# Threshold attention and a hash-routed mixture of experts: one of the seven products by quarters, sums kept in PSUM, attention's transfers in other steps

## The chip, the cores and the metric

The kernel runs on one core of a Trainium2 chip. The metric is the device time of one execution in microseconds (us); less is better. The engines are TensorE (PE in the profile; its weight loads PEld), VectorE (DVE), ScalarE (ACT), GpSimd (POOL) and SyncE (SP), which here only issues DMAs.

## The reference

Two blocks in a row, in fp32. Attention with a threshold: B=8, H=8, S=576, D=64; only scores within tau of a row's largest count. Its output, 4608 rows of 512, goes through a layer of 8 experts, each 512 to 1024 with ReLU and back to 512. The token's id alone says which expert gets it.

```python
scores = scale * np.matmul(q, k.transpose(0, 1, 3, 2))
thresh = np.max(scores, axis=-1, keepdims=True) - tau
scores = np.where(scores >= thresh, scores, -1000000000.0)
attn = np.exp(scores - np.max(scores, axis=-1, keepdims=True))
attn = attn / (np.sum(attn, axis=-1, keepdims=True) + 1e-09)
x = np.matmul(attn, v)                        # then (B,H,S,D) to (B*S, H*D)
expert_idx = token_ids * np.int64(2654435761) % np.int64(E)
for e in range(E):
    mask = expert_idx == e
    h = np.maximum(x[mask] @ w1[e], 0.0)
    out[mask] = h @ w2[e]
```

## The kernel before, in words

**Attention** (0 to some 480 us) goes over 32 pairs of heads (p), each in five steps (s = 0 to 4), in one hand-written order: a loop over n = 5p + s (L710) issues the work of several pairs at once. For step n it scores (`score`, PE, L235), negates with a row maximum (`negate`, DVE, L246, and on POOL the threshold `thr`, L253), exponentiates (`expo`, ACT, L260) and masks (`mask`, DVE, L271). Two steps later the weights are transposed on PE (`turn_w`, L282) and copied by ACT (`put_wT`, L303). The product with v follows for the pair before (`av_part`, L313). For a finished pair, POOL adds epsilon to the row sums at s = 1 (`add_eps`, `rec`, L343), DVE takes the reciprocal at s = 2 (L740), and at s = 0, two pairs late, `put_xm` multiplies (DVE, L352) and SP writes the rows to x_scratch in DRAM by three DMAs (L358, L363). Each engine runs its own instructions in this order.

Between these run POOL's indirect transfers. `scatters` (L542) writes the 36 columns of token ids to their slots, one at each step but s = 1. Once the slots are known, `fetch_early` gathers 15 blocks of the first expert's rows (`gather`, L119: 5 tiles of rows, three of the four column blocks of 128 each), at steps 3 and 4 and at the start of step 0 (L714, L803), from n > G0 = 130. The fourth column block is gathered in five transfers after the last pair. SP loads the first experts' weights at s = 2 of pairs 20, 22, 24 and 26.

**Experts** (some 500 us to the end) take one of eight after the other, with capacities of 544 tokens (expert 0), 576 (1 to 4) and 600 (5 to 7). Expert 0's first layer runs during the end of attention (`early_h`, L640; `late_h`, L658 to L664, of which the last tile, fo = 5, lies in a buffer of `ps_m`). All other layers are products of 2 by 2 blocks computed with seven products instead of eight (`seven`, L931): layer 1 in two groups g of output rows (`layer1`), layer 2 at once (`layer2`). `left` and `right` make the sums of blocks on DVE (L858, L861). A product (L941) is 4 (layer 1) or 8 (layer 2) matmuls into each half of a pair of PSUM banks; each matmul shows as two records of the profile[...]. `bank2` hands out four such pairs of banks in turn. Each product is followed by one operation that empties its banks: ACT copies the first to SBUF (`p1`, L951), and DVE adds each of the others to a running sum in SBUF (`u2`, `u3`, `u4`) or to an output (L861); ReLU is ACT's (L948).

After certain products `side1` (layer 1) or `side2` (layer 2) issues the work around: sums for the next layer, squares of the gathered rows (`turn_x`, DVE transposes and then 16 DMAs on SP that move them to xT), `fetch` of the expert after next (POOL gathers), the outputs (`put_squares`: a DVE transpose, L1033, then a POOL scatter of each square, L1042) and the weight loads. After each of those transfers `pause` makes POOL copy a small tile twice (L1027). The last expert's layer 2 covers 480 of its tokens; the last 120 are `last_tile` (L990, L994), with `put_out` (L1009 to L1021) in between.

The tile pools count buffers; the order of instructions on each engine is the program's own (`manual_schedule`), and waits between engines are derived from who writes and reads a tile.

Of the kernel before, what the change touches and what calls it, by code (L numbers as in the profile page):

```python
# [9 lines left out]
FP32 = mybir.dt.float32  # L10
# [3 lines left out]
AF = mybir.ActivationFunctionType  # L14
# [6 lines left out]
def kernel(  # L21
# [12 lines left out]
    nc = tc.nc  # L34
# [109 lines left out]
    with tc.tile_pool(name="a_q", bufs=1) as a_q, \  # L144
# [525 lines left out]
        LAST = NS * NP  # L670
        G0 = NS * ((HP - 1) * B + 2)
        early = [(kt, hp) for kt in range(KT) for hp in range(HP - 1)]
# [15 lines left out]
        with tc.manual_schedule():  # L688
# [21 lines left out]
            for n in range(LAST + NS + 1):  # L710
                p, s = divmod(n, NS)
                m = n - 2
                if s == 0:
                    fetch_early(n)  # L714
                if s == 0 and p + 2 < NP:
# [81 lines left out]
                if 0 < n <= LAST:  # L797
                    for j in range(heads(n - 1)):
                        mask(n - 1, j)
                if s != 1 and placed:  # L800
                    next(scatter_pieces, None)
                if s > 2:
                    fetch_early(n)  # L803
                if n == LAST:
                    fill(1)
# [21 lines left out]
    with tc.tile_pool(name="m_x", bufs=1) as m_x, \  # L827
         tc.tile_pool(name="m_o", bufs=3) as m_o, \
         tc.tile_pool(name="m_s", bufs=1) as m_s:
# [7 lines left out]
        nc.gpsimd.memset(oT[:, :, CAP:SL], 0.0)  # L837
        o_end = m_x.tile([P, DIN], FP32, name="o_end")
        mark = m_x.tile([P, 1], FP32, name="mark")
        w1_s = m_s.tile([P, 3, C2, F2], FP32, name="w1_s")  # L840
        CH = CAP // 2
        x_s = m_s.tile([P, 3, C2, CH], FP32, name="x_s")
        w2_s = m_s.tile([P, 3, FH, D2], FP32, name="w2_s")
        h_s = m_s.tile([P, 3, FH, CH], FP32, name="h_s")
        halves = [m_s.tile([P, 2, CH], FP32, name=n) for n in ("p1", "u2", "u3", "u4")]
        CHL = 32 * (NB - 4) // 2

        ps_m = ctx.enter_context(tc.tile_pool(name="ps_m", bufs=2, space=PSUM))
        turn = [0]

        def bank2():
            turn[0] ^= 1
            if turn[0]:
                return ps_sc.tile([P, 2, 512], FP32, name="sc")
            return ps_m.tile([P, 2, 512], FP32, name="bank2")

# [30 lines left out]
        def w2_sums(e):  # L887
            t = triple(w2_s, 0, FH)
            return t if e == E - 1 else [dealt(x, C2) for x in t]

# [18 lines left out]
        def sums_w2(e):  # L909
            s1 = None  # L910
            if e == E - 1:
                spare = w_pool.tile([P, CO, F], FP32, name="w1_sb")
                s1 = w_tiles["s1"] = spare[:, :, 0:D2]
            return left(*w2_blocks(e, w_tiles[e, 2]), w2_sums(e), s1)

# [9 lines left out]

        def seven(a, a_s, b, b_s, m0, outs, relu, after):

            (a11, a12, s1, a22), (s2, s3, s4) = a, a_s
            (b11, t1, b21, b22), (t2, t3, t4) = b, b_s
            c11, c12, c21, c22 = outs  # L930
            n_k, width, dealt_out = a11.shape[1], b11.shape[2], len(a11.shape) == 4  # L931
            p1, u2, u3, u4 = (t[:, :, 0:width] for t in halves)

            def product(x, y):
                ps = bank2()
                for i in range(2):
                    c0 = m0 + P * i
                    for c in range(n_k):
                        lhsT = (x[:, c, :, i] if dealt_out else
                                x[:, c, c0:c0 + P])  # L940
                        nc.tensor.matmul(ps[:, i, 0:width], lhsT=lhsT, rhs=y[:, c],  # L941
                                         start=c == 0, stop=c == n_k - 1)
                return ps[:, :, 0:width]

            def out(c, ps, u, step):
                add(c, ps, u)()
                if relu:
                    nc.scalar.activation(c, c, AF.Relu)  # L948
                after(step)

            nc.scalar.copy(p1, product(a11, b11))  # L951
            out(c11, product(a12, b21), p1, 0)
            add(u2, product(s2, t2), p1)()
            after(1)
            add(u3, product(s3, t3), u2)()
            after(2)
            out(c21, product(a22, t4), u3, 3)
            k5 = product(s1, t1)
            add(u4, k5, u2)()
            out(c22, k5, u3, 4)  # L960
            out(c12, product(s4, b22), u4, 5)

        def layer1(e, side):

            w, half = w_tiles.pop((e, 1)), caps[e] // 2
            for g in range(NG):
                outs = [h_0[:, FH * i + 2 * g:FH * i + 2 * g + 2, half * k:half * k + half]
                        for i in range(2) for k in range(2)]
                seven(w1_blocks(w), triple(w1_s, 0, C2), x_blocks(e), triple(x_s, 0, C2, half), 2 * P * g,
                      outs, True, lambda step: side(g, step))  # L970

        def layer2(e, side):

            w, half = w_tiles[e, 2], half2(e)
            outs = [oT[:, C2 * i:C2 * i + C2, half * k:half * k + half]
                    for i in range(2) for k in range(2)]
            a = w2_blocks(e, w)
            if e == E - 1:
                a[2] = w_tiles["s1"]
            seven(a, w2_sums(e), h_blocks(0, FH, half),  # L980
                  triple(h_s, 0, FH, half), 0, outs, False, side)

        def last_tile(middle):

            w, o_sb, idx = w_tiles[E - 1, 2], o_end, gidx[:, KT - 1:KT]
            rows = CAP - 2 * CHL
            for c0, c1 in ((0, DIN - P), (DIN - P, DIN)):
                ps = bank2()
                for fo in range(FO):
                    nc.tensor.matmul(ps[0:rows, 0, 0:c1 - c0], lhsT=h_0[:, fo, 2 * CHL:CAP],  # L990
                                     rhs=w[:, fo, c0:c1], start=fo == 0, stop=fo == FO - 1)
                    if (c0, fo) == (0, FH - 1):
                        middle()
                nc.scalar.copy(o_sb[0:rows, c0:c1], ps[0:rows, 0, 0:c1 - c0])  # L994
            put_rows(o_sb[0:rows], idx[0:rows])

        def put_out(e, *groups):
# [14 lines left out]
            for tr, kts in zip(trs, groups):  # L1012
                for i, kt in enumerate(kts):
                    rows = rows_of(kt)
                    o_sb = m_o.tile([P, DIN], FP32, name="o_sb")
                    dst = o_sb[0:rows].rearrange("p (c r q) -> p r c q", c=CO, r=2)
                    src = tr[0:rows, :, D2 * i:D2 * i + D2].rearrange("p r (c q) -> p r c q", c=CO)
                    if e == E - 1 and kt % 2:
                        nc.vector.tensor_copy(dst, src)
                    else:  # L1020
                        nc.scalar.copy(dst, src)  # L1021
                    put_rows(o_sb[0:rows], gidx[0:rows, kt:kt + 1])

        def pause():

            for _ in range(2):
                nc.gpsimd.tensor_copy(stok_odd[:], stok[:])  # L1027

# [48 lines left out]
        with tc.manual_schedule():  # L1077
            run(sums_w2(0), 4)
            fill(18)
            late_h(lambda fo: (ps_sc.tile([P, 2, 512], FP32, name="sc") if fo in (2, 4) else  # L1080
                               ps_m.tile([P, 2, 512], FP32, name="bank2")))
            fetch(1)
            run(sums_h(0, 0, FH), 4)

        with tc.manual_schedule():
            for e in range(E):
                more = e + 1 < E
                turns = turn_x(e + 1) if more else []

                if e > 0:  # L1090
                    w2_work, h_work = sums_w2(e), sums_h(e, 0, 2)

                    def side1(g, step):
                        if g == 0:
                            run(w2_work)
                            if step == 0:
                                put_squares(e - 1, 1)
                        else:
                            run(h_work)
                        if step > 2:  # L1100
                            run(turns, 1 if g == 0 else 2)

                    layer1(e, side1)
                    run(sums_h(e, 2, FH), 4)
                x_work = (sums_w1(e + 1) + sums_x(e + 1)) if more else []

                def side2(step):
                    if step == 0:
                        run(turns, len(turns))
                    else:  # L1110
                        run(x_work, 2)
                    if step == 2 and e + 2 < E:
                        fetch(e + 2)
                    if step == 4 and e + 2 < E:
                        load_w1(e + 2)
                    if more and step == 3:
                        put_squares(e, 0)
# [23 lines left out]
        with tc.For_i(0, n_ov, 1) as it:  # L1141
# [23 lines left out]
            for fo in range(FO):  # L1165
                nc.tensor.matmul(o_ps[:, 0], lhsT=h_0[:, fo, 0:P], rhs=w2_sb[:, fo],
                                 start=(fo == 0), stop=(fo == FO - 1))
            o_sb = m_o.tile([P, DIN], FP32, name="o_sb")
            nc.scalar.copy(o_sb[:], o_ps[:, 0])
# [35 lines left out]
```

## Time and profile before

| | us |
|---|---|
| median of 3 runs | 918.26 |
| lowest, highest | 918.19, 919.33 |
| profiled execution, its own time | 926.27 |
| its span, first to last instruction | 924.6 |
| outside the span | 1.7 |

The profiled execution takes 8.0 us more than the median, so durations are read from it and the result is compared with the median. The granted TensorE clock is 0.999 over the span.

A row of the timeline gives start, duration, engine, line, operation, output and inputs with their shapes, and in brackets how long the engine stood before it and what released it. Neighbouring instructions of one kind are drawn together (x16). A row of busy time by stage gives the length of the stage and the busy time of PE, PEld, DVE, ACT and POOL in it, then the clock, the share of the DMA engines and GB/s. Matmul ends are modelled in the profile, so products are timed here from start to start.

The stages (busy us):

| stage, us | PE | DVE | ACT | POOL |
|---|---|---|---|---|
| 0 to 460, attention | 449.45 | 444.82 | 390.48 | 214.93 |
| 460 to 500, change-over | 39.72 | 19.00 | 10.34 | 9.64 |
| 600 to 650, experts | 50.00 | 36.65 | 5.39 | 38.86 |
| 850 to 900, experts | 50.00 | 32.43 | 7.38 | 40.33 |
| 900 to 925, the end | 17.71 | 3.95 | 1.91 | 9.81 |

### The profile page before, as it was taken

Reading aid. Unit: us, or ns where it says so; the run is one execution under the profiler, and the core shown is the slowest. Engines: PE = TensorE matmul, PEld = TensorE weight load, DVE = VectorE, ACT = ScalarE, POOL = GpSimd, SP = SyncE. Lnnn points to the kernel's source line nnn. Section 1 sums busy time; section 2 is a strip of 40 time slices with the busy share of each in tenths; the row PEclk is TensorE's granted clock in tenths of the full one; section 3 lists DMA queues with packets and bytes.
Section 4 is the critical chain, followed back from the end, with each engine's and each line's share of the span. In section 5 each row is a group of like instructions: output and inputs, shape, how many; then the busy total and the mean of one; then the engine's idle time right before and its main releaser. Section 6 shows DMA issues by size and latency. Waiting matters only on the chain.

```text
span 924.6 us, 21039 instructions
## 1 busy us (share of the span) xinstructions
PE 906.9 (98%) x7495; PEld 661.6 (72%) x7495; DVE 759.9 (82%) x1654; ACT 457.3 (49%) x741; POOL 550.1 (59%) x842
## 2 busy tenths in 40 slices
PE   7999999999999999999999999999999999999997
PEld 4666666656666666565668879788887978879785
DVE  8999999999999999999945696867768685786741
ACT  6888888888888898788922020110202011020210
POOL 4233432456666623446414588787787877878773
PEclk9999999999999999999999999999999999999999
DMA  7454463554545668734011636445252543522001
GB/s 175 95 146 123 107 152 96 134 134 101 124 100 149 167 164 220 209 96 108 16 33 56 195 118 185 136 125 196 63 199 90 170 155 90 218 61 67 28 28 62
DMA packets 114777, 113.13 MB, mean 122 GB/s; under 512 B 32475, under 2 KB 89315, under 8 KB 114672
## 3 DMA queue, kind: packets, MB, share of 16 engines
q1 hardware_dynamic: 105168, 92.64, 37.0%
q0 software_dynamic: 9072, 18.91, 6.6%
q8 instruction: 61, 1.00, 0.4%
q14 instruction: 44, 0.36, 0.1%
q10 hardware_dynamic: 432, 0.21, 0.1%
HBM read 81.99 MB, written 21.44 MB: 112 GB/s over the span
## 4 chain that ended last, share of the span: by engine, by line
PE 83%; POOL 6%; issue 4%; DVE 3%; ACT 2%; DMA 1%; SPq 0%; POOLq 0%; DVEq 0%; ACTq 0%
PE bank L941 18%; PE av L313 18%; PE sc L941 18%; PE sc L235 14%; PE tr L282 11%; POOL out_dram L1042 4%; PE sc L640 3%; POOL stok_odd L1027 2%; PE av L282 1%; DVE ns L246 1%; DVE w L271 1%; ACT w L260 1%; DMA k_sb<-in_k_dram 1%; ACT wT_b L303 1%; PE bank L658 0%
## 5 line engine op out<-in xcount | busy, mean ns | idle before, releaser
L260 ACT ACTIVATE w<-ns,nmx 128x576 f32<-128x576 f32 x288 | 220.4, 776 | 28.6 <-DVE ns L246 27.9
L271 DVE SCALAR_TENSOR_TENSOR w<-ns,thr,w 128x576 f32<-128x576 f32 x288 | 225.7, 816 | 0.0
L253 POOL TENSOR_SCALAR thr<-nmx,drop 128x2 f32<-128x2 f32 (+1 forms) x160 | 104.4, 652 | 188.9 <-DVE ns L246 179.1
L246 DVE TENSOR_SCALAR_CACHE_REDUCE ns<-sc 128x576 f32<-128x576 f32 x288 | 205.7, 746 | 8.5 <-PE sc L235 7.7
L235 PE MATMUL sc<-k_sb,q 64*128 64x288 f32 (+1 forms) x1280 | 178.2, 422 | 1.1 <-DVE ns L246 0.6
L282 PEld LDWEIGHTS tr<-ident,w 64*128 64x128 f32 x2624 | 105.6, 138 | 96.9 <-ACT wT_b L303 35.3
L1042 POOL DMA_INDIRECT out_dram<-o_q,qidx x127 | 139.7, 1100 | 57.8 <-issue 49.2
L282 PE MATMUL tr<-ident,w 64*128 64x64 f32 x2624 | 139.2, 230 | 7.7 <-ACT wT_b L303 4.8
L1027 POOL COPY stok_odd<-stok 128x152 int32<-128x152 int32 x314 | 139.9, 445 | 10.0
L948 ACT ACTIVATE h<-h 128x576 f32<-128x576 f32 (+1 forms) x56 | 38.8, 693 | 142.8 <-DVE h L861 142.0
L235 PEld LDWEIGHTS sc<-k_sb,q 64*128 64x128 f32 (+1 forms) x1280 | 92.2, 177 | 23.5 <-DVE ns L246 9.8
L313 PE MATMUL av<-wT_a,v 128*64 128x320 f32 (+1 forms) x704 | 100.4, 418 | 0.2
L303 ACT COPY wT_a<-tr 128x512 f32<-128x512 f32 (+1 forms) x128 | 81.7, 638 | 20.6 <-PE tr L282 20.1
L303 ACT COPY wT_b<-tr 128x512 f32<-128x512 f32 (+1 forms) x128 | 81.3, 635 | 18.2 <-PE tr L282 10.2
L313 PE MATMUL av<-wT_b,v 128*64 128x256 f32 x640 | 83.2, 389 | 0.0
L313 PEld LDWEIGHTS av<-wT_a,v 128*64 128x64 f32 x704 | 43.7, 136 | 29.0 <-DVE xm L352 0.7
L951 ACT COPY p<-bank 128x576 f32<-128x576 f32 (+2 forms) x11 | 7.0, 634 | 107.5 <-PE bank L941 102.5
L313 PEld LDWEIGHTS av<-wT_b,v 128*64 128x64 f32 x640 | 40.2, 136 | 18.8 <-issue 0.7
L119 POOL DMA_INDIRECT xg<-x_scratch,gidx_x x35 | 41.8, 1193 | 19.2 <-issue 9.3
L542 POOL DMA_INDIRECT slot_scratch<-tok,slot_i x36 | 44.9, 1247 | 9.5 <-issue 7.6
L951 ACT COPY p<-sc 128x576 f32<-128x576 f32 (+2 forms) x11 | 7.0, 637 | 84.7 <-PE sc L941 79.8
L941 PE MATMUL bank<-h,w_sb 128*128 128x288 f32 (+3 forms) x192 | 48.1, 404 | 0.0
(198 smaller groups left out, 1402.4 us busy)
## 6 DMA issues: line engine op xcount, KB each, us to landing
w_sb<-in_moe_w_dram SPq DMA_DIRECT2D x16, 2048.0 KB
q<-in_q_dram SPq DMA_DIRECT2D x62, 288.0 KB
v<-in_v_dram SPq DMA_DIRECT2D x32, 256.0 KB
x_scratch<-xm SPq DMA_DIRECT2D x32, 256.0 KB
xT<-xq SPq DMA_DIRECT2D x84, 80.0 KB
k_sb<-in_k_dram SPq DMA_DIRECT2D x31, 144.0 KB
k_sb<-in_k_dram SPq DMA_DIRECT2D x32, 112.0 KB
x_scratch<-xg SPq DMA_DIRECT2D x9, 256.0 KB
```

The costliest lines, as they stand in the source:

```text
L235: nc.tensor.matmul(sc[out_rows, i, 0:S2], lhsT=q_sb[rows, h, q0:q1], rhs=k_sb[rows, h], start=True, stop=True)
L246: nc.vector.tensor_scalar(out=ns[:].rearrange("p (i s) -> p i s", i=2), in0=sc[:, :, 0:S2], scalar1=-1.0, scalar2=None, op0=ALU.mult, op1= ...
L253: nc.gpsimd.tensor_scalar(out=thr[:, 0:j + 1], in0=stats[n][0][:, 0:j + 1], scalar1=drop[:], scalar2=None, op0=ALU.add)
L260: nc.scalar.activation(w, nss[n, j][:], AF.Exp, bias=stats[n][0][:, j:j + 1], scale=-1.0)
L271: nc.vector.scalar_tensor_tensor(out=w, in0=nss.pop((n, j))[:], scalar=stats[n][1][:, j:j + 1], in1=w, op0=ALU.is_le, op1=ALU.mult, accum_ ...
L282: nc.tensor.transpose(dst[:, r, 64 * c:64 * c + 64], src[rows, c0:c0 + P], ident[rows, rows])
L303: nc.scalar.copy(dst, tr[:, :, 0:64 * n_c].rearrange("p r (c q) -> p r c q", c=n_c))
L313: nc.tensor.matmul(av[64 * j:64 * j + 64, g, c0:c1], lhsT=v_sb[:, c, 64 * j:64 * j + 64], rhs=wT[g][:, i, c0:c1], start=(c == 0), stop=stop)
L542: nc.gpsimd.indirect_dma_start(out=slot_dram[c % 2][:, :], out_offset=bass.IndirectOffsetOnAxis(ap=slot_i[:, c:c + 1], axis=0), in_=tok[:, ...
L941: nc.tensor.matmul(ps[:, i, 0:width], lhsT=lhsT, rhs=y[:, c], start=c == 0, stop=c == n_k - 1)
L1027: nc.gpsimd.tensor_copy(stok_odd[:], stok[:])
L1042: inst = nc.gpsimd.indirect_dma_start(out=rows[:, :], out_offset=bass.IndirectOffsetOnAxis(ap=idx, axis=0), in_=o_sb, in_offset=None, boun ...
```

## The change

**Quarters.** For experts 1 to 7 the second product of each layer, a12·b21, is itself computed with seven products of its quarters (class `Quarters`), in both groups of layer 1 at once. It takes the place of one product in layer 2 and of one in each group of layer 1. Inner sums of the weights (`wi_s`, 128x256 each) and of the inputs (`bi_s`) are made on DVE by the same `left` and `right`. Since layer 2's weights lie in an interleaved order, ACT first copies the block into four quarters (`copy_quarters`, `w2_q`). Expert 0 keeps the plain second product.

**Sums in PSUM.** A class `Seven` takes the place of `seven`. The running sums stay in the banks: u2 = p1 + s2·t2, u3 = u2 + s3·t3 and c21 = u3 + a22·t4 are added by matmul in bank x, and s1·t1 and s4·b22 in bank z. Where a partial sum is needed elsewhere, ACT copies it out before the next matmul adds to the bank (`p1`, `u2`, `mid`); c21 goes to its place by ACT, with ReLU in layer 1. DVE is left with three additions in place of seven for one `Seven`, and one more for c11 where the second product comes by quarters. Four pairs of banks are held from the start of the experts (`banks`) and are handed to the sums by name; the order of the products, and what `side1` and `side2` issue between them, is written anew. Expert 0's layer 2 opens in banks[3], which is the buffer of `late_h`'s last tile.

**Attention's transfers.** Scatters go at steps 0 to 3, not at 0 and 2 to 4. Gathers of the first expert go at steps 2 and 3, from n > G0 = 125, and what remains of the 15 goes all at once at n = 155 (the last pair's step 0); three are left by then.

**Smaller parts.** `pause` copies once and not twice. The output tiles of the end are the buffers of the gathered rows (xg), and the pool m_o is gone. The first squares of an output go out at `side2`'s step 4 and not 3, those of expert 0 in the first layer of expert 1.

```diff
-        G0 = NS * ((HP - 1) * B + 2)
+        G0 = NS * ((HP - 1) * B + 1)
...
-                if s == 0:
-                    fetch_early(n)
...
-                if s != 1 and placed:
+                if s < NS - 1 and placed:
                     next(scatter_pieces, None)
-                if s > 2:
+                if s in (2, 3):
                     fetch_early(n)
+                if n == LAST - NS:
+                    while early:
+                        fetch_early(n)
...
-        def seven(a, a_s, b, b_s, m0, outs, relu, after):
...
-            nc.scalar.copy(p1, product(a11, b11))
-            out(c11, product(a12, b21), p1, 0)
-            add(u2, product(s2, t2), p1)()
-            after(1)
-            add(u3, product(s3, t3), u2)()
-            after(2)
-            out(c21, product(a22, t4), u3, 3)
-            k5 = product(s1, t1)
-            add(u4, k5, u2)()
-            out(c22, k5, u3, 4)
-            out(c12, product(s4, b22), u4, 5)
+        class Seven:
...
+            def keep_p1(self):
+                nc.scalar.copy(self.p1, self.x)
...
+            def u2_sum(self):
+                products(self.x, self.a[4], self.b[4], False)
+                nc.scalar.copy(self.u2, self.x)
...
+            def u3_sum(self, keep):
+                products(self.x, self.a[5], self.b[5], False)
+                if keep:
+                    nc.scalar.copy(self.mid, self.x)
+
+            def c21(self):
+                products(self.x, self.a[3], self.b[6], False)
+                if self.relu:
+                    nc.scalar.activation(self.outs[2], self.x, AF.Relu)
+                else:
+                    nc.scalar.copy(self.outs[2], self.x)
+
+            def c12(self, mid=None):
+                products(self.z, self.a[6], self.b[3], False, mid)
+                self.out(self.outs[1], self.z, self.u2)
...
+        class Quarters:
...
+            def p1_p2(self):
+                products(self.x, self.a[0], self.b[0], True)
+                nc.scalar.copy(self.p1, self.x)
+                products(self.y, self.a[1], self.b[2], True)
+
+            def c11(self):
+                add(self.outs[0], self.y, self.p1)()
+
+            def p5_u2(self):
+                products(self.z, self.a[2], self.b[1], True)
+                nc.scalar.copy(self.p5, self.z)
+                products(self.x, self.a[4], self.b[4], False)
+                nc.scalar.copy(self.u2, self.x)
+
+            def c12_c22(self):
+                products(self.z, self.a[6], self.b[3], False)
+                add(self.outs[1], self.z, self.u2)()
+                products(self.x, self.a[5], self.b[5], False)
+                add(self.outs[3], self.x, self.p5)()
+
+            def c21(self):
+                products(self.x, self.a[3], self.b[6], False)
+                nc.scalar.copy(self.outs[2], self.x)
...
+            q = quarters_of(e, 1, *banks[1:])
+            g0, g1 = group(0, banks[0], banks[2]), group(1, banks[1], banks[3])
+            g0.first()
+            g0.keep_p1()
+            side(0)
+            q.p1_p2()
+            q.c11()
+            g0.u2_sum()
+            side(1)
+            q.p5_u2()
+            g0.s1_t1(True)
+            side(2)
+            q.c12_c22()
+            side(3)
+            g0.u3_sum(False)
+            q.c21()
+            g0.c22(g0.x)
+            side(4)
+            g0.c12()
+            g0.c11(g0.p1)
+            g1.first()
...
+            g1.c11(g1.x)
+            g1.relus()
+            g0.c21()
+            side(6)
+            g1.u2_sum()
...
+            o = Seven(a, w2_sums(e), h_blocks(0, FH, half), triple(h_s, 0, FH, half), 0, outs,
+                      False, *((banks[0], banks[1]) if e else (banks[3], banks[2])))
+            o.first()
+            o.keep_p1()
...
+            q = quarters_of(e, 2, *(banks[i][:, 0:1] for i in (2, 3, 3)))
+            q.p1_p2()
+            q.c11()
+            run(inner_b(second_blocks(e, 2)[1]), 4)
+            o.u2_sum()
+            q.p5_u2()
+            side(0)
+            o.u3_sum(True)
+            side(1)
+            q.c12_c22()
+            o.s1_t1(False)
+            side(2)
+            q.c21()
+            o.c11(o.p1)
+            o.c22(o.z)
+            o.c21()
+            side(3)
+            o.c12(lambda: side(4))
...
         def pause():
 
-            for _ in range(2):
-                nc.gpsimd.tensor_copy(stok_odd[:], stok[:])
+            nc.gpsimd.tensor_copy(stok_odd[:], stok[:])
```

## The prediction

> **What bounds the kernel now.** I read the busy shares and the chain of the page first, then busy time by stage, then the timeline at the places that the edits touch. On the page:
>
> ```profile
> PE 906.9 (98%) x7495; PEld 661.6 (72%) x7495; DVE 759.9 (82%) x1654; ACT 457.3 (49%) x741; POOL 550.1 (59%) x842
> PE 83%; POOL 6%; issue 4%; DVE 3%; ACT 2%; DMA 1%; SPq 0%; POOLq 0%; DVEq 0%; ACTq 0%
> L1027 POOL COPY stok_odd<-stok 128x152 int32<-128x152 int32 x314 | 139.9, 445 | 10.0
> ```
>
> TensorE is 98% busy and 83% of the chain. POOL's copies are 140 us of work, but they are not what ends the program, as the last fence shows. Busy time by stage (columns: sum, then PE, PEld, DVE, ACT, POOL) says how exclusive TensorE is in the experts:
>
> ```profile
> 600.00:650.00 50.00, 50.00 (x208) 42.84 (x207) 36.65 (x43) 5.39 (x8) 38.86 (x57) 1.00 0.48 151
> 850.00:900.00 50.00, 50.00 (x213) 41.20 (x213) 32.43 (x39) 7.38 (x11) 40.33 (x66) 1.00 0.09 28
> ```
>
> 50.00 of 50 us: no product waits there, DVE has a quarter of its time free and ACT nearly all. So TensorE time removed from the experts is time removed from the program, unless a new wait takes its place. How a product is priced, and how soon a bank is emptied:
>
> ```profile
> 608.63 0.74 DVE L861 TENSOR_TENSOR h<-sc,u 128x576 f32<-128x576 f32 x1
> ...
> 612.99 4.04 PE L941 MATMUL bank<-h,w_sb 128*128 128x288 f32 x16
> ...
> 613.24 0.64 ACT L951 COPY p<-sc 128x576 f32<-128x576 f32 x1 [2.46 <-issue]
> ...
> 616.87 1.38 PE L941 MATMUL sc<-h_s,w_s 128*128 128x288 f32 x5
> ```
>
> A layer-2 product starts at 612.99, the next at 616.87: 3.88 us for 16 records, 0.2425 us each. The copy of the product before starts 0.25 us after its successor does and takes 0.64. The sum that ended at 609.37 had begun 1.5 us after its bank was full (607.17), behind other DVE work: today that delay costs nothing.
>
> In attention POOL's gathers matter:
>
> ```profile
> 388.43 1.02 POOL L119 DMA_INDIRECT xg<-x_scratch,gidx  x1 [0.30 <-issue]
> 389.49 0.81 POOL L253 TENSOR_SCALAR thr<-nmx,drop 128x1 f32<-128x1 f32 x1
> 389.89 0.58 ACT L303 COPY wT_b<-tr 128x512 f32<-128x512 f32 x1 [1.81 <-PE sc L235]
> 390.53 0.39 PEld L282 LDWEIGHTS tr<-ident,w 64*128 64x128 f32 x10 [2.03 <-ACT wT_b L303]
> 390.53 0.52 PE L282 MATMUL tr<-ident,w 64*128 64x64 f32 x10 [1.58 <-ACT wT_b L303]
> ```
>
> The transposes that ACT needed were issued at 387.46, but its copy starts only at 389.89, 0.4 us after the end of a gather that was issued at the start of step 0, right behind one from the end of step 4, and TensorE stands for 1.58 us. The same happens at 434.9 (1.64). The end:
>
> ```profile
> 915.80 1.91 PE L990 MATMUL sc<-w_sb,h 128*120 128x128 f32 x16
> ...
> 917.75 0.27 ACT L994 COPY o_end<-sc 120x128 f32<-120x128 f32 x1 [1.27 <-PE sc L990]
> 918.32 1.03 POOL L1042 DMA_INDIRECT out_dram<-o_end,gidx  x1 [0.81 <-issue]
> ```
>
> TensorE's last product, one copy, one transfer: POOL has had nothing else to do for 0.8 us.
>
> **What the Trainium skill says.** (1) "TensorE: Matmul & The Clock Gate", section "Step-by-step: what each phase is for": back to back, a matmul costs its moving columns, and weights are loaded ahead of it. The trace agrees: 300 columns take 0.2525 us, 288 take 0.2425, 272 take 0.229, 128 take 0.109 (L990), near 0.842 ns a column with no visible fixed part. (2) The same page, "LDWEIGHTS (loading the stationary operand)": a load takes its columns over 1.2, so an estimate of 107 ns for 128 columns. The trace's nearest is L990: 120 columns keep up with 0.109 us. (3) "PSUM — Partial Sum Buffer", "PSUM: the matmul accumulator": a matmul that does not open a group adds to what lies in the bank, and a synchronised read in between is allowed. The kernel before never does this, so its trace cannot confirm it; it is what makes part 2 possible, and the synchronisation is its price. (4) "DMA: Bandwidth & Descriptors", "Anatomy of one DMA — SWDGE (gpsimd) path": some 2 us of every transfer is completion. The trace's case is on SP and longer: x_scratch is issued at 477.83 and the gather behind it starts at 481.39.
>
> **The change part by part.** The sum is made on the profiled execution: 926.27 us, span 924.6, 1.7 around it. The median of the runs is 918.26, 8.0 less, and I carry that difference over unchanged.
>
> *1. Quarters.* From expert 1 on, a12·b21 of each layer (3.88 us at 288 columns; two groups of 1.94 in layer 1) becomes seven products of an eighth of it: 28 records x 144 columns x 0.842 = 3.395. Saved 0.485; 0.505 at 300 columns; 0.404 at 240. Widths are 288 for experts 1 to 4, 300 from 5, 240 in the last layer 2: 8 x 0.485 + 5 x 0.505 + 0.404 = **6.8 us**. Bounds: if the weight load sets the pitch, 0.107 (estimate) to 0.117 (0.109 x 128/120) is still under 0.121, so I take 6.8 in full. The new sums (DVE, for each layer 4 of weights, 4 of inputs, 4 of outputs, at about 0.2 to 0.45 by their widths) stand against four removed sums of 0.75 in each of three sevens: about 8 us added and 8.4 removed in 54 us, so DVE stays at some 75%. ACT gains a copy of w2 and up to nine copies, about 15 us in 54, free time.
>
> *2. Sums kept in PSUM.* A product that adds to a bank must wait until ACT has copied the partial sum out: 0.25 + 0.64 + 0.06 restart (ACT copy to PE in attention, 0.06) = 0.95, or 1.00 with a weight load not taken ahead. At three places of an expert (u2 of layer 1's first group, u2 and u3 of layer 2) only two quarter products lie between, 2 x 0.485 = 0.97. Elsewhere a product of 1.94 or more lies between. Bounds per place 0 (a wait cannot gain) to 0.1; I take 0.03 x 21 = **0.6 us lost**. Behind the wait stand all later products, since TensorE keeps their order. Banks that DVE must empty: I laid the new order out with these durations and find the narrowest covers at 0.5 (bank of the first quarter product), 0.9 (second group's first product) and 1.0 us; I take nothing, and price the contrary below.
>
> *3. Expert 0.* Its layer 2 now opens in the bank of the last late_h tile, which DVE reads at 501.83 for 0.72; TensorE would start at 502.6 and not at 501.63: 1.0. The transfers of xT to expert 1 on SP move back by 2.2 us, since the squares run behind more sums; they take 10.5 us to issue and land about 0.4 before the need (0 to 2). The squares of expert 0 now lie in layer 1 of expert 1 ahead of a quarter sum: 0.3. Together **1.3 lost** (1 to 3). In the last expert, cover is 0.81 against a chain of 0.86 to 0.93, and 120-column records may be bound by weights at 0.109 to 0.117, not 0.101: **0.3 lost** (0.2 to 0.6).
>
> *4. One pause.* 157 copies x 0.445 = 70 us leave POOL. It sets no end in the experts, so nothing; squares, gathers and output tiles only come free earlier.
>
> *5. Attention transfers.* Scatters leave the end of step 4 and get a place in step 1; gathers leave step 4 and the start of step 0. Starts of xm give 13.9 us for a plain pair; the nine pairs with scatters take 4.0 more in sum. I credit **2.5** (0 to 4), as the one now in step 1 stands behind rec and thr on POOL, ahead of nothing urgent. The gather pairs take 16.3, 13.9, 14.7 and 15.2, 4.5 over; with gathers in steps 2 and 3 alone I credit **3.5** (2 to 4.5). Against that, three gathers now stand together at the start of the last pair, and the first must wait for x_scratch of two pairs before. In the kernel before:
>
> ```profile
> 447.96 0.82 DVE L352 TENSOR_TENSOR xm<-av,rec 128x640 f32<-128x640 f32 x1
> ...
> 450.50 0.54 POOL L343 TENSOR_SCALAR rec<-rs 128x9 f32<-128x9 f32 x2
> ...
> 452.27 0.21 DVE L740 RECIPROCAL rec<-rec 128x10 f32<-128x10 f32 x1
> ```
>
> xm ends at 448.8; three DMAs on SP (the tail's 477.83 to 481.39 shows up to 3.6 us until a gather) put the first gather at 451.7 to 452.3. Three at the tail's pitch of about 1.6 end near 456.6. thr of the next step and rec of the pair queue behind them on POOL, so rec comes at 457.2 and DVE's reciprocal, due at 452.27, with the masks behind it, waits **5.0** (2.4 to 6); DVE is 97% busy in attention and TensorE follows it. Net **+1.0 gained** (-3 to +5). load_w1, load_w2 and load_pair keep their places on SP.
>
> Sum: 6.8 - 0.6 - 1.3 - 0.3 + 1.0 = 5.6. Profiled execution about 920.7; median 918.26 - 5.6 = **912.7**.
>
> **The rivals.** *DVE late at the banks (slower).* A bank that TensorE needs again is emptied by a DVE sum, and DVE runs in order; the trace shows such sums starting up to 1.46 us after the bank is full, behind a sum of 1.24. With fixed banks that is TensorE time at the first quarter product, at the second group's u2 and at the quarter outputs. It decides from (5.6 + 1.8)/7 = 1.06 us an expert. At two such places of 0.8 each, 11.2 us: 918.26 - 5.6 + 11.2 = **923.9**. For it: DVE at 73%, nearly 30 sums an expert in a new order; against it: covers of 0.5 to 1.0 in my layout, and long sums dealt out step by step.
> *The gathers of the last pair are hidden.* If masks can run ahead or the transfers land early, the 5.0 stays away: 918.26 - 10.6 = **907.7**. Against: reciprocal stands in order ahead of the masks.
> *The products do not shrink.* If 28 short records are paced by weight loads at 0.139 us (3.88/28), part 1 gives nothing: 918.26 + 1.2 = **919.5**. Against: L990's 0.109.
> *Attention loses.* Low credits (2) and 6 at the last pair: 4 worse than nothing, 5 worse than forecast, **917.7**.
>
> **How the numbers follow.** A measurement here can tell about 0.2% (1.84 us) from no change. Likeliest case 912.7, with 909.5 to 915.5 for the bounds of parts 2, 3 and 5: 0.53. Gathers hidden, 906 to 909.5: 0.20. Attention loses or products do not shrink, 916.4 to 920.1: 0.13. DVE late or another wait of that size, over 920.1: 0.14. So faster 0.73, same 0.13, slower 0.14. The range runs from 906.5 to 919.5, leaving out the slower case and little else.
>
> **What would show it.** Right: quarter records every 0.121 us, PE busy about 6.8 us less in the experts, gaps of under 0.1 us ahead of u2, one gap near 1 us at 502, no gap at the starts of pairs 26 to 30, one of 3 to 5 us near 452 to 457 on DVE. Wrong: PE gaps released by DVE sums in each expert, quarter records above 0.13 us, or a last pair without a stall. The forecast fails most easily in part 5, where the loss is an extrapolation.

## The result and the profile after

The changed kernel takes 920.28 us (median of 20 runs, 918.83 to 923.09), the kernel before beside it 918.43 (20 runs, 917.62 to 919.68). The ratio is 1.0019 (95% interval 1.0012 to 1.0026): 1.7 us slower (1.1 to 2.4). Forecast were 5.6 us less.

The page of the changed kernel, its busy shares, its chain and its pauses:

```profile
PE 901.5 (98%) x7663; PEld 669.6 (73%) x7663; DVE 758.9 (83%) x1720; ACT 513.9 (56%) x848; POOL 488.5 (53%) x685
PE 50%; POOL 28%; issue 15%; DVE 2%; ACT 2%; SPq 1%; DMA 1%; POOLq 1%; DVEq 0%; ACTq 0%
L1235 POOL COPY stok_odd<-stok 128x152 int32<-128x152 int32 x157 | 69.5, 443 | 0.6
```

TensorE is busy for 5.4 us less than in the profile before, and ACT for 57 us more. Part of the 5.4 is not less work: a later profile of the kernel before (before_third, below) has TensorE busy for 904.2 us and not 906.9, so 2.7 are left. POOL lost 70 us of its copies. The chain's shares have moved to POOL, but that is only the path by which the chain was followed: the time by stage (sum, PE, PEld, DVE, ACT, POOL) still has TensorE at 50.00 of 50.

```profile
600.00:650.00 50.00, 50.00 (x234) 44.18 (x233) 37.12 (x54) 14.11 (x24) 33.37 (x42) 1.00 0.48 151
850.00:900.00 50.00, 50.00 (x248) 42.56 (x247) 25.85 (x37) 13.33 (x25) 29.00 (x38) 1.00 0.08 25
```

The span of this profile is 917.2 us, and 1.6 lie around it: 918.83, the least of its 20 runs and 1.4 below their median. Against the profile before (span 924.6) it seems 7.4 us faster, while the runs say 1.7 slower. That contradiction is the subject of the experiments. The large wait of the changed kernel is where the prediction put it, at the start of the last pair:

```profile
440.76 1.15 SPq L363 DMA_DIRECT2D x_scratch<-xm  x2
...
443.98 1.10 POOL L119 DMA_INDIRECT xg<-x_scratch,gidx  x1 [3.93 <-DMA x_scratch<-xm]
...
446.69 1.01 POOL L119 DMA_INDIRECT xg<-x_scratch,gidx  x1 [0.30 <-issue]
...
447.77 0.53 POOL L343 TENSOR_SCALAR rec<-rs 128x9 f32<-128x9 f32 x2
...
448.34 0.22 DVE L738 RECIPROCAL rec<-rec 128x10 f32<-128x10 f32 x1 [4.45 <-POOL rec L343]
...
449.26 2.01 PE L235 MATMUL sc<-k_sb,q 64*128 64x288 f32 x8 [3.24 <-DVE ns L246]
```

Read it from the bottom: TensorE waits 3.24 us for DVE, DVE waits 4.45 us for POOL's rec, and three gathers on POOL stand ahead of rec, the first of them for 3.93 us behind the transfer of xm.

### The profile page after: what moved, and what is told of

The parts are those of the page before. It is cut to its first block, busy times and chain, and to the rows that moved or that the text cites. A ratio compares the mean times of both kernels' runs of the same rounds, so it can differ in the third digit from the quotient of the medians.

```text
span 917.2 us, 21463 instructions
## 1 busy us (share of the span) xinstructions
PE 901.5 (98%) x7663; PEld 669.6 (73%) x7663; DVE 758.9 (83%) x1720; ACT 513.9 (56%) x848; POOL 488.5 (53%) x685
## 4 chain that ended last, share of the span: by engine, by line
PE 50%; POOL 28%; issue 15%; DVE 2%; ACT 2%; SPq 1%; DMA 1%; POOLq 1%; DVEq 0%; ACTq 0%
PE av L313 18%; POOL out_dram L1250 17%; PE sc L235 15%; PE tr L282 10%; POOL stok_odd L1235 7%; POOL xg L119 4%; PE sc L640 3%; PE av L282 1%; SPq L1280 1%; ACT w L260 1%; DMA k_sb<-in_k_dram 1%; DVE ns L246 1%; POOLq L1250 0%; PE sc L940 0%; PE bank L940 0%
## 5 line engine op out<-in xcount | busy, mean ns | idle before, releaser
L1250 POOL DMA_INDIRECT out_dram<-o_q,qidx x127 | 147.5, 1161 | 114.6 <-DVE o_q L1241 81.5
L253 POOL TENSOR_SCALAR thr<-nmx,drop 128x2 f32<-128x2 f32 (+1 forms) x160 | 101.1, 632 | 176.4 <-DVE ns L246 167.2
L1235 POOL COPY stok_odd<-stok 128x152 int32<-128x152 int32 x157 | 69.5, 443 | 0.6
L940 PE MATMUL bank<-h,w_sb 128*128 128x288 f32 (+4 forms) x248 | 62.0, 402 | 0.0
L940 PEld LDWEIGHTS bank<-h,w_sb 128*128 128x128 f32 x248 | 58.7, 290 | 0.5
L940 PE MATMUL sc<-h_s,w_s 128*128 128x288 f32 (+2 forms) x224 | 56.6, 406 | 0.0
L964 ACT ACTIVATE h<-h 128x576 f32<-128x576 f32 (+1 forms) x42 | 29.0, 692 | 41.3 <-DVE h L867 41.2
L119 POOL DMA_INDIRECT xg<-x_scratch,gidx_x x35 | 44.7, 1278 | 12.3 <-DVE xq L1272 5.3
```

The costliest lines, as they stand in the source:

```text
L119: nc.gpsimd.indirect_dma_start(out=dst, out_offset=None, in_=src, in_offset=bass.IndirectOffsetOnAxis(ap=idx, axis=0), bounds_check=src.sh ...
L253: nc.gpsimd.tensor_scalar(out=thr[:, 0:j + 1], in0=stats[n][0][:, 0:j + 1], scalar1=drop[:], scalar2=None, op0=ALU.add)
L940: nc.tensor.matmul(ps[:, i], lhsT=lhsT, rhs=y[:, c], start=start and c == 0, stop=c == len(lhsTs) - 1, skip_group_check=not start)
L1250: inst = nc.gpsimd.indirect_dma_start(out=rows[:, :], out_offset=bass.IndirectOffsetOnAxis(ap=idx, axis=0), in_=o_sb, in_offset=None, boun ...
```

## Experiments

There are two theories. *A*: the experts give their 4 us, the moved transfers give nothing, because the long pairs of the first profile are not in the timed runs, and the three gathers of the last pair cost 5 to 6. *B*: the moved transfers do gain what the first profile shows, and something else, in the experts, loses it in timed runs. The kernels of one set were timed on one chip, each beside the same runs of the kernel before. Each set had another chip: 11, 13 and 8 on record. For the first measurement no chip is on record.

### First set: the two halves of the change apart

**before_again**: no edit. 

> The kernel before, unchanged, for a second profile. Theory A (the 8 us by which the first profiled execution of before exceeded its runs were stalls of that one execution, in the pairs with gathers and scatters; they hardly exist in the timed runs): span near 917, the pairs with gathers at 13.9 to 14.3 and not 16.3 and 15.2. Theory B (these stalls are there in every execution): span near 924 again with the same long pairs. Both: ratio 1.000 within 0.001.

**before_attn**: the kernel before with

```diff
-        G0 = NS * ((HP - 1) * B + 2)
+        G0 = NS * ((HP - 1) * B + 1)
-                if s == 0:
-                    fetch_early(n)
-                if s != 1 and placed:
+                if s < NS - 1 and placed:
-                if s > 2:
+                if s in (2, 3):
                     fetch_early(n)
+                if n == LAST - NS:
+                    while early:
+                        fetch_early(n)
```

> The kernel before with the three attention edits alone (steps of scatters, steps of gathers, the rest of the gathers at the last pair). Theory A: they give nothing and the three gathers at n = 155 cost 4.5 us of DVE standing plus 1.5 us of lower TensorE clock: about 924.4, ratio 1.0065. Theory B: 8 us gained, 4.5 to 6 lost: about 916, ratio 0.997.

**after_old_attn**: the changed kernel with these lines turned back. 

> The changed kernel with the attention transfers at the steps of before. Theory A: only the experts' 4 us are left: about 914.3, ratio 0.9955 to before. Theory B: the attention's net gain is lost again and the experts cost something in timed runs: about 922, ratio 1.004.

**after_spread**: the changed kernel with

```diff
-                if s in (2, 3):
+                if s in (2, 3) or s == 1 and p in (28, 29, 30):
                     fetch_early(n)
-                if n == LAST - NS:
-                    while early:
-                        fetch_early(n)
```

> The changed kernel with the last three gathers not together at n = 155 but one each at step 1 of pairs 28, 29 and 30, so that all are out before the last pair. Theory A: the stall of 4.5 us and the slow clock behind it are gone: about 914, ratio 0.995. Theory B: 4.5 us less than the changed kernel's 920.3, about 915.8, ratio 0.997, but before's attention would still be 8 us slower in its own profile.

| kernel | median, us | ratio to before | 95% interval |
|---|---|---|---|
| before, in this set | 924.89 | | |
| before_again | 925.84 | 1.001 | 1.0002 to 1.0018 |
| before_attn | 926.91 | 1.0025 | 1.0014 to 1.0036 |
| after_old_attn | 921.39 | 0.9966 | 0.9953 to 0.9979 |
| after_spread | 918.51 | 0.9929 | 0.9913 to 0.9944 |

This time the kernel before took 924.9 and not 918.4, and so the set answers neither theory as written. What it tells is this: the experts alone gain (0.9966); the attention edits as a whole lose (1.0025); and the harmful one among them is that the last three gathers stand together (0.9929 without it). A pair's length is read from one start of xm to the next. In the profile of before_again the nine scatter pairs are together 3.8 us longer than nine plain pairs of 13.9, and the four gather pairs 3.0; the first profile had 4.0 and 4.5. So the long pairs are there where the kernel takes 925 us. They are not made by profiling: the profiled execution took 924.59, as its set's other runs did.

### Second set: the stall of the last pair, and the layers

**after_again**: the changed kernel once more. 

> The changed kernel, unchanged, beside the kernel before on one chip, so that the parts can be summed there. If the parts add up: where before takes 918.4, ratio 1.002 again; where before takes 924.9 (its gather and scatter pairs lengthened), the old steps cost more and the ratio falls to about 0.999, since 0.9966 for the changed kernel with the old steps and 1.0025 for the attention edits alone multiply to 0.999.

Before 918.0 here; 919.51, ratio 1.0019 (1.0012 to 1.0025), the same as at first.

**after_early3**: the changed kernel with

```diff
             for n in range(LAST + NS + 1):
                 p, s = divmod(n, NS)
                 m = n - 2
+                if n == LAST - NS:
+                    while early:
+                        fetch_early(n)
...
                 if s in (2, 3):
                     fetch_early(n)
-                if n == LAST - NS:
-                    while early:
-                        fetch_early(n)
```

> The changed kernel with its three gathers of n = 155 at the beginning of that step, ahead of put_xm of pair 29 in the order, so that they need not wait for its DMAs to x_scratch; still three in a row. If the wait for x_scratch is the cost (3.9 of the 4.45 us for which DVE stood): 0 to 1 us of standing is left, TensorE keeps its clock, about 5 us faster than the changed kernel. If the gathers' own time on POOL is the cost: it stays within 1.5 us of the changed kernel.

915.33 us, ratio 0.9969 (0.9958 to 0.998), 4.2 less than after_again. The timeline of its last pair:

```profile
438.35 1.37 POOL L119 DMA_INDIRECT xg<-x_scratch,gidx  x1 [0.17 <-issue]
439.43 0.82 DVE L352 TENSOR_TENSOR xm<-av,rec 128x640 f32<-128x640 f32 x1
440.02 1.01 POOL L119 DMA_INDIRECT xg<-x_scratch,gidx  x1 [0.30 <-issue]
441.34 1.25 POOL L119 DMA_INDIRECT xg<-x_scratch,gidx  x1 [0.31 <-issue]
...
443.03 0.88 POOL L343 TENSOR_SCALAR rec<-rs 128x9 f32<-128x9 f32 x2
...
444.09 0.37 SPq L358 DMA_DIRECT2D x_scratch<-xm  x1
```

There are still three gathers in a row, but rec comes 4.7 us earlier. Now xm's transfer waits for the gathers, and no engine is seen to wait for it. From the xm of pair 29 to that of pair 30 are 13.32 us, in the changed kernel 18.37: 5.05 more. In before_third (third set) they are 13.33. So the price was the wait for x_scratch and not the gathers' own time. In time the edit gave 4.2 us; the 1 us by which it stays behind the kernels of the third set (0.9969 against 0.9957 and 0.9959) is within the intervals.

**after_plain2**: the changed kernel with

```diff
-            if e == 0:
-                o.second(banks[0])
+            if e >= 0:
+                o.second(banks[2 if e else 0])
```

In this order the first squares of an expert's output leave before its c21 block is written, so that block of the output is not the reference's. 

> The changed kernel with layer 2's second product of experts 1 to 7 plain again (one product of 128x288 and no quarters), sums still in PSUM. By the prediction's price of a quartered layer (0.485 and two waits of 0.03): 3 us slower than the changed kernel. By what its trace shows (layer 2 took 27.03 us, of which 0.32 are four delayed second records, against 27.16 for seven products of 3.88): only 0.9 us slower.

928.99 us, ratio 1.0112 (1.0098 to 1.0127): 9.5 us more than after_again, a miss of both figures, mostly because the edit brought a wait of its own: c21 now comes last, and the next layer's first product needs its bank.

```profile
PE sc L940 <- ACT oT L999: 6.6, 6, 1.2
```

The products tell more than the total. Without that wait layer 2 of expert 2 takes 27.16 us in this kernel, 7 x 3.88, and 27.03 with quarters in the changed one: 0.13 gained, not 0.485. That reading rests on one trace of each.

**after_swap**: after_spread with

```diff
-            q.c21()
-            o.c11(o.p1)
             o.c22(o.z)
             o.c21()
+            q.c21()
+            o.c11(o.p1)
             side(3)
             o.c12(lambda: side(4))
```

> The changed kernel with the last three gathers at step 1 of pairs 28 to 30, and with the last quarter product of layer 2 moved behind a22·t4, ahead of s4·b22. Behind that quarter then stand weights of w_s (loads of about 196 ns) and not of w_sb (308 ns). If the 0.108 us by which the second record of the next product is late comes from the long weight load behind short records: it is gone at this place (0.02 left), 0.09 x 7 = 0.6 us, on top of the 6 us from the gathers. If it comes from the accumulation into the bank: it stays.

939.94 us, ratio 1.0234 (1.0221 to 1.0248). The expectation's premise was mistaken: from this change on, s4 is written in place into w_sb, so the last product has the same strided weights as the one before, and the late record stayed (the product took 3.99 us). The kernel lost time for another reason:

```profile
PE bank L937 <- DVE oT L864: 15.8, 6, 2.7
```

And the timeline of one of the six:

```profile
631.56 2.10 PE L937 MATMUL sc<-xT,w_sb 128*128 128x288 f32 x8
...
633.48 2.21 DVE L1238 STREAM_TRANSPOSE o_q<-oT 128x1152 f32<-128x1152 f32 x1
...
635.54 0.73 DVE L864 TENSOR_TENSOR oT<-bank,u 128x576 f32<-128x576 f32 x1
...
636.33 0.76 PE L937 MATMUL bank<-xT,w_sb 128*128 128x144 f32 x4 [2.66 <-DVE oT L864]
```

The bank of c12 is full at 631.56, when the next product starts; its addition begins at 635.54, behind the sums for the next expert and the squares' transpose, all of which had to wait for the late c11. This is the prediction's slower rival, made by hand: 2.56 to 2.67 us at one bank in each of six experts, 15.8 in sum. That is not all of the 25 us that this kernel takes more than after_spread_again (third set). By the trace's record of the granted clock, it fell to half for 3.4 us after five of the six waits, and TensorE had work then: an estimate of 1.7 us each, 8.5 in sum. A stage with one such fall (the clock is the column after the busy times; without a fall it is 1.00):

```profile
600.00:650.00 50.00, 47.34 (x215) 41.61 (x214) 32.35 (x46) 11.44 (x20) 28.59 (x35) 0.97 0.46 148
```

### Third set: what is the attention worth where before takes 918?

**before_third**: no edit. 

> The kernel before, for a profile beside the others of this call, since its time was 918.0 to 918.4 in two sets of runs and 924.9 in another. If its pairs with scatters and gathers are what differs: with a median near 918 they take hardly more than 13.9 us each (sum of excess under 2), with a median near 925 they show 7 to 8 us of excess as in the first profile; the experts take 390.1 from expert 1 on in either.

**before_spread**: before_attn with after_spread's edit. 

> The kernel before with attention's new steps but the last three gathers at step 1 of pairs 28, 29, 30 in place of the last pair: what the moved transfers are worth by themselves. Theory A at a median of before near 918: within 1.5 us of before; at one near 925: 4 us faster (0.9929/0.9966). Theory B: 6 us faster in either.

**after_spread_again**: after_spread. 

> The changed kernel with the last three gathers at step 1 of pairs 28 to 30. Experts' 4.0 us and what before_spread shows: at a median of before near 918, 0.9950; near 925, 0.993.

**after_old_again**: after_old_attn. 

> The changed kernel with the attention transfers at the steps of before: the experts' part alone, 4.0 us by the traces, ratio 0.9957 wherever it runs.

| kernel | median, us | ratio to before | 95% interval |
|---|---|---|---|
| before, in this set | 918.28 | | |
| before_third | 918.27 | 1.0002 | 0.9994 to 1.0011 |
| before_spread | 918.73 | 1.0007 | 0.9998 to 1.0016 |
| after_spread_again | 914.87 | 0.9959 | 0.9945 to 0.9973 |
| after_old_again | 914.27 | 0.9957 | 0.9943 to 0.997 |

Where the kernel before takes 918, this is theory A on every line. In the profile of before_third (span 916.6) the scatter pairs are together 0.1 us shorter than plain ones and the gather pairs 0.3 longer. The place shown in the prediction looks like this in this execution:

```profile
382.52 1.35 POOL L119 DMA_INDIRECT xg<-x_scratch,gidx  x1 [0.17 <-issue]
...
383.65 0.59 ACT L303 COPY wT_b<-tr 128x512 f32<-128x512 f32 x1
384.18 1.02 POOL L119 DMA_INDIRECT xg<-x_scratch,gidx  x1 [0.30 <-issue]
384.29 0.46 PEld L282 LDWEIGHTS tr<-ident,w 64*128 64x128 f32 x10 [0.16 <-ACT wT_b L303]
384.42 0.47 PE L282 MATMUL tr<-ident,w 64*128 64x64 f32 x10
```

The same two gathers with the same durations stand at the same point; but ACT copies at 383.65, 0.5 us after the start of the transposes it needs and ahead of the second gather's start, and TensorE goes on. In the first profile ACT came only after that gather's end. It is the same program in another execution, and the difference is 1.58 us of standing TensorE at one place. All profiles of the set on chip 11 have lengthened pairs, 6.8 and 7.1 us in sum with the transfers of before (before_again, after_old_attn) and 1.8 and 2.0 with the moved ones (after_spread, before_attn); in those from chips 13 and 8 it is 0 to 1.3 us. So the chip, or what goes with it, is a cause that was not tested: no chip on record has a second set. What delays ACT stays open.

## Why the prediction was wrong

**The step that failed** is part 5's credit: "I credit **2.5**" for the scatters and "**3.5**" for the gathers. Where the kernel before takes 918, the moved transfers are worth 1.0007 (0.9998 to 1.0016), that is nothing. The stalls were real in the profiled execution, but they are what made it 8.0 us longer than the median: 4.0 and 4.5 us of excess are 8.5, and in before_third, whose profile took 918.19, they are 0.2. The prediction named the 8.0 ("I carry that difference over unchanged"): with it the median was already free of these stalls, and then 6.0 us of them were taken out a second time. One addition would have raised the suspicion. In the set at 924.9 the credit has something to it: after_spread against after_old_attn is 0.9929/0.9966, 3.4 us.

**The loss at the last pair** was right in mechanism; that the size came out too was in part luck. Forecast were 5.0 us of standing DVE; it stood for 4.45, and 5.05 were lost from xm to xm. It was set against a gain that was not there. A piece was left out: the Trainium skill, "TensorE: Matmul & The Clock Gate", "Part 1: The HAM clock gate (the "warmup" mystery)", says that TensorE's clock falls after an idle window of some 3.4 us. In these traces less was enough: here TensorE stood for 3.24 us, and the granted clock was 0.70 in the stage of 5 us from 450 on; in after_swap waits of 2.56 to 2.67 us were followed by a fall five times out of six:

```profile
445.00:450.00 5.00, 1.76 (x22) 0.86 (x18) 1.66 (x6) 0.88 (x3) 2.85 (x6) 0.96 0.04 8
450.00:455.00 5.00, 5.00 (x44) 3.06 (x42) 4.34 (x13) 4.16 (x8) 1.45 (x2) 0.70 0.02 3
```

What the fall alone costs was not tested by a run. From DVE's reciprocal to the xm of pair 30 are 9.53 us here and 8.80 in after_early3, where the clock stayed at 1.00: an estimate of 0.7 us.

**Parts 1 to 3, the experts**: 4.6 forecast, 3.9 measured (after_old_again, 0.9957); by the traces 390.12 us from expert 1 to TensorE's end become 386.07. The sum came near, its terms less so:

- *Pitch*, the time from one record to the next. It is 0.1225 us at 144 columns and not 0.121: 6.8 become 6.3. Weight loads did not set it there. In the last expert 120 columns take 0.110 and not 0.101, which part 3 had allowed for.
- *Waits for ACT* before a bank is added to: 0.02 at u2 and 0.08 at u3 in layer 2, within the bounds that were forecast.
- *A term that was missing.* The third and fourth delays of a layer 2 are no waits. After records of 144 columns, the second record of a product whose weights lie strided in w_sb comes 0.108 us late. One such place (PEld are the loads, PE the records; each row begins with start and duration):

```profile
618.80 0.65 PE L940 MATMUL sc<-bi_s,wi_s 128*128 128x144 f32 x4
...
619.17 3.93 PEld L940 LDWEIGHTS bank<-h,w_sb 128*128 128x128 f32 x16
619.29 4.15 PE L940 MATMUL bank<-h,w_sb 128*128 128x288 f32 x16
```

  These loads take 309 ns, those of the contiguous quarters 190. In the last expert, whose weights are not interleaved, they take 190 too, and the same second record is 0.010 late. That adding to a bank delays it is ruled out by the same trace: the product above opens its bank, and the u3 product of layer 1 at 586.66 adds to one, has contiguous weights and is not late. So all points to the strided load, but no run changed the load alone; the one meant to (after_swap) left it as it was. The prediction could have seen the long loads. It reckoned with an estimate of 107 ns a load, while the trace before has these (shortest, median and longest in ns):

```profile
L941 PEld LDWEIGHTS sc<-h,w_sb x192: 190/308/320, 501.4 to 905.3; 128*128 128x128 f32 x192
```

  There, behind records of 288 columns, they cost nothing. Two places of 0.108 in six experts are 1.3 us. Of the 6.3 us 4.05 were left in the traces: some 2.2 us were lost where 0.9 had been allowed.
- *Expert 0*: 1.3 forecast, 0.07 measured (25.96 to 26.03). Its layer 2 starts at 498.05 without a wait, while DVE reads the last late_h tile only from 498.25 on. So banks[3] cannot be that tile's buffer, and the section on the change says this wrongly. The transfer to expert 1 was in time.

**Part 4** was right as far as the traces go: 70 us less of pauses on POOL and no effect on the end; TensorE's last record is still followed by one copy and one transfer. No run tested it alone.

**The sum**, measured: experts -3.9, moved transfers +0.6 (none, within the interval), last pair +5.0: +1.7, which is the result. The 5.0 is the traces' figure; the times give 4.2 (after_early3 against after_again) to 5.5 (1.0019 against after_spread_again's 0.9959). Of the rivals, "Attention loses" (917.7) had the right mechanism: it let attention lose 4 us, and some 5.6 were lost, more than the experts gain. "The products do not shrink" (919.5) came nearest in number, and by luck: the products did shrink. "The gathers of the last pair are hidden" (907.7) is what after_spread and after_early3 make true at the last pair, but without the credit of 6.0 that gives 914.87 and 915.33. "DVE late at the banks" does not occur in the changed kernel: no bank waits for DVE there, though after_swap shows how near it is. The prediction's own bounds for the net of part 5 (-3 to +5) were also narrower than its terms, which give -4 to +6.1.

**The better version** is the changed kernel with the attention of before, or with its last gathers at step 1: 914.27 and 914.87 against 918.28, 0.4% faster than the kernel before.

## What to carry to other kernels

When the profiled execution is longer than the median, find where it is longer before pricing anything: stalls that make up the difference are not there to be won in the timed runs. A second profile, whose own time agrees with the median, shows them by their absence. A transfer that reads a buffer just written waited here for the whole write (3.93 us), and so did all that was queued behind it on its engine; moving it ahead of the write by a few lines was worth 4 us. A product split into smaller ones must be priced with its neighbours: the product behind short records lost 0.108 us here, most likely because they no longer hid a long weight load.

## What was not expected of the hardware

A load of 128x128 weights at a stride of four elements took 309 ns, one at a stride of two 196, a contiguous one 190; behind 288-column records all are hidden (0.2425 us a record in each case), behind 144-column records the first goes with a delay of 0.108 us. TensorE's granted clock fell to half for 3.4 us after waits as short as 2.57 us. And the same program took 918.0 to 918.4 us in three sets of runs and 924.9 in another, with the difference in ACT's start after TensorE's transposes near POOL's indirect transfers.
